# Row maxima of causal attention: which query tiles share a PSUM bank, and in which order their matmuls and searches are issued

## The chip, the cores and the metric

The kernel runs on one core of one Trainium2 chip. The metric is the device time of one execution in microseconds (us), lower is better. Engines are named as in the profile: PE (TensorE matmuls), PEld (TensorE weight loads), DVE (VectorE), ACT (ScalarE), POOL (GpSimd) and SP (SyncE, which issues the DMAs). A PSUM bank holds 512 fp32 columns on 128 partitions; PE writes its results there, DVE and ACT read them.

## The reference, cut to what matters

A block of 2048 tokens by 1024 channels: adaptive layer norm, gated infini-attention with 32 heads of 32 channels, a residual, a second layer norm, a token-mixing MLP, a second residual. The change lies in the attention, which works on four segments of 512 tokens:

```python
for s in range(N):                                   # N = 4 segments, L = 512
    qs, ks, vs = q[:, :, s], k[:, :, s], v[:, :, s]
    logits = jnp.einsum("bhqd,bhkd->bhqk", qs, ks) * scale + mask   # causal
    p = _softmax(logits, axis=-1)
    a_dot = jnp.einsum("bhqk,bhkd->bhqd", p, vs)
    ...                                              # memory read, gate, memory update
```

A softmax row needs the maximum of its logits. The kernel finds it in a pass of its own, for each head and segment: 512 queries, each against the keys up to its own position.

## The kernel before, in words

**Stages.** The first 70 us load inputs and build the first normed segment. From there to about 1035 us runs the attention: a loop over 32 iterations (two passes, eight groups of four heads, two segments each) with four heads in each, so 128 heads in all. The rest is the output product (L733) and the MLP (L863), which the change doesn't touch.

**The loop of the attention (L631 to L655).** Step `n` emits, in this order: `scores(n)`, `maxima(n + 3)`, `values(n - 1)`, and one of four pieces of `project` for a later iteration; beside these come loads, weight splits and other work from a table of due steps (`todo`). `project` computes keys and values (L196) and queries (L204) in fp32 split into a high and a low part, and stacks them by DMA into the tiles `sk`. `scores` computes the transposed logits (L476 to L483) and their exponentials. `values` multiplies by the values (L505) and finishes on DVE (L508 to L513).

**`maxima` (L431 to L456).** For one head the 512 queries are taken in four tiles of 128. Tile i needs the keys of tiles 0 to i: its matmul (L441) has 128·i + 128 columns, so 128, 256, 384 and 512. After each matmul one DVE operation (L442) adds the causal mask, writes the sum back in place and leaves the row maximum in a column of `mx`; the profile shows it as a CUSTOM_DVE operation followed by a short READ_ACCUMULATOR. I call it the search of the tile. Before, the code asks for three tiles of the PSUM tag `s1`, which has two banks: x holds query tile 0 in columns 0 to 127 and query tile 2 in columns 128 to 511, y holds query tile 1, and z query tile 3. The order written down is matmul 0, search 0, matmul 2, search 2, matmul 1, search 1, matmul 3, search 3. After every second head the maxima of both are transposed on PE (L448), negated and split (L450, L451), and four DMAs (L455) put them as two extra rows into `sk`, where the matmuls of `scores` subtract them.

**What sets the order on the chip.** The program is laid out ahead of time by a planner. It takes the instructions in program order as priority, uses its own estimates of their durations, and writes a fixed queue for each engine; a later instruction whose inputs it plans to be ready may be put ahead of an earlier one that it plans to wait. Banks of one tag are handed out by the planner too, to the next tile that asks as soon as it plans one free. On the chip each engine works its queue strictly in order, and an instruction waits where its input or its bank isn't ready yet. Two instructions of different engines on one bank are kept in program order, even where their columns differ.

Other users of the tag `s1`: one in two of the transposes of the first segments (L221, before the loop), the first query projection, and the MLP, long after the loop. The tags `pj` (2 banks), `s2` (2), `pv` (1) and `ms` (1) hold the projections, the scores, the values and the small results.

Of the kernel before, what the change touches and what calls it, by code (L numbers as in the profile page):

```python
# [12 lines left out]
ALU = mybir.AluOpType  # L13
# [16 lines left out]
LEADP, LEADS, NSK = 8, 3, 8  # L30
# [12 lines left out]
LEADS = 3  # L43


def attention_and_mlp(ctx, tc, x, wq, wkv, wo, beta, w1, b1, w2, b2, c, wm_a, wm_b, out):
    nc = tc.nc
    V, A, G, T, SY = nc.vector, nc.scalar, nc.gpsimd, nc.tensor, nc.sync
# [27 lines left out]
    def bank(tag, bufs, name):  # L76
        return psum.tile([P, 512], F32, tag=tag, bufs=bufs, name=name)
# [5 lines left out]
    mask = top.tile([P, L], BF16, name="mask")  # L83
# [194 lines left out]
    for ct in range(NK):  # L278
        for part in range(2):
# [9 lines left out]
            else:  # L289
                for k in range(NK):  # L290
                    T.matmul(scale_ps[:, ct:ct + 1], wm[:, P * k:P * k + P], sc[:, k:k + 1], start=(k == 0),
                             stop=(k == NK - 1), skip_group_check=True)
# [138 lines left out]
    def maxima(t, h):  # L431
        d = st[t]
        if h % 2 == 0:
            d["mx"] = b.tile([P, 2, 4], F32, tag="mx", bufs=2, name=f"mx{t}_{h}")
        mx = d["mx"]
        q, k = d["sk", h][0:96, 0], d["sk", h][0:96, 1]
        x = bank("s1", 2, f"sx_{t}_{h}")
        y = bank("s1", 2, f"sy_{t}_{h}")
        z = bank("s1", 2, f"sz_{t}_{h}")
        for i, o in ((0, x[:, 0:128]), (2, x[:, 128:512]), (1, y[:, 0:256]), (3, z)):  # L440
            T.matmul(o, q[:, 128 * i:128 * i + 128], k[:, 0:128 * i + 128], start=True, stop=True)  # L441
            marks[4 * t + h - LEADS, "V"] = V.tensor_tensor_reduce(  # L442
                o, o, mask[:, 384 - 128 * i:], 1.0, -3.0e38, op0=ALU.add, op1=ALU.max,
                accum_out=mx[:, h % 2, i:i + 1])
        if h % 2 == 0:
            return
        ps = bank("ms", 1, f"nmps{t}_{h}")
        T.transpose(ps[0:8, 0:128], mx.rearrange("p a b -> p (a b)"), ident)  # L448
        nt = [b.tile([8, P], F32R, tag=f"nt{i}", bufs=2, name=f"nt{i}_{t}_{h}") for i in range(2)]
        A.activation(nt[0], ps[0:8, 0:128], AF.Copy, scale=-1.0)  # L450
        V.scalar_tensor_tensor(nt[1], ps[0:8, 0:128], -1.0, nt[0].bitcast(F32), op0=ALU.mult, op1=ALU.subtract)  # L451
        for hh in range(2):
            sk = d["sk", h - 1 + hh]
            for part in range(2):
                SY.dma_start(sk[96 + part:97 + part, 0].bitcast(F32).rearrange("p (b n) -> p b n", n=128),  # L455
                             nt[part][4 * hh:4 * hh + 4].bitcast(F32))  # L456

    marks = {}
# [172 lines left out]
    for n in range(-LEADS, 4 * NI + VL):  # L631
        at(scores, n)
        at(maxima, n + LEADS)
        at(values, n - VL)
        m = n + LEADP
        if 0 <= m + 4 < 4 * NI:
            t = (m + 4) // 4
            if its[t][:2] not in W:
                with tc.issue_after(last_sk[0, 3].ins):
                    load_w(its[t][1], its[t][0])  # L640
        if m >= 8:
            at(project, m)
        if 59 <= m < 67:
            seg, ct = 2 + (m - 59) // 4, 2 * ((m - 59) % 4)
            reload_h(seg, ct)
            reload_h(seg, ct + 1)
        if 4 * NI - 5 <= m < 4 * NI + 3:
            i = m - 4 * NI + 5
            for c in (2 * (i % 4), 2 * (i % 4) + 1):
                wop[c, i // 4] = new_page(f"wo{c}_{i // 4}")  # L650
                if c < 5 or i < 4:
                    SY.dma_start(wop[c, i // 4].bitcast(F32), wos[c, i // 4])
        for f, engines in todo.pop(n, ()):
            with behind(n, engines):
                f()  # L655
# [58 lines left out]
    def product(tt):  # L714

        r = wr_.tile([P, NK, P], F32, tag="otr", bufs=1, name=f"otr{tt}")
        SY.dma_start(r, oT[:, :, P * tt:P * tt + P].rearrange("g p n -> p g n"))
        os_ = ws_.tile([P, 2, D], F32R, tag="ots", bufs=2, name=f"ots{tt}")
        for j in range(2):
            split(os_[:, :, 512 * j:512 * j + 512], r[:, 4 * j:4 * j + 4].rearrange("p a b -> p (a b)"), A, V)  # L720
        x1 = w.tile([P, D], F32, tag="x1", bufs=2, name=f"x1_{tt}")
        load = SY.dma_start(x1, x[P * tt:P * tt + P])
        if tt == 1:
            with tc.issue_after(load.ins):
                for c in range(5, NK):
                    SY.dma_start(wop[c, 1].bitcast(F32), wos[c, 1])

        def half(nh):
            ps = bank("pj", 2, f"po{tt}_{nh}")
            n = 0  # L730
            for ct in range(NK):
                for i, j in ((0, 0), (0, 1), (1, 0)):
                    T.matmul(ps, os_[:, i, P * ct:P * ct + P], wop[ct, nh][:, j], start=(n == 0), stop=(n == 3 * NK - 1))  # L733
                    n += 1
            c0, c1 = 512 * nh, 512 * nh + 512
            V.scalar_tensor_tensor(x1[:, c0:c1], ps, 1.0, x1[:, c0:c1], op0=ALU.mult, op1=ALU.add,
                                   accum_out=x1s[:, 2 * tt + nh:2 * tt + nh + 1])
            if nh:
                kept[tt] = SY.dma_start(x1d[tt], x1)

        return half
# [49 lines left out]
    for products, tt in (((0, 1), 0), ((2,), 1), ((3, 4, 8), 8), ((9,), 9), ((10,), 2), ((11,), 10), ((12,), 3),  # L791
# [5 lines left out]
        for i in products:  # L797
            if i > 1:
                f = product(i)
# [284 lines left out]
```

## Time and profile before

| | us |
|---|---|
| median of 3 runs | 2254.03 |
| lowest and highest of them | 2251.84, 2257.36 |
| the profiled execution | 2248.92 |
| its span, first to last instruction | 2247.2 |
| PE busy in it | 2195.4 |
| DVE busy | 1671.5 |
| ACT busy | 1145.6 |
| POOL busy | 748.6 |

How to read the views: a row of grouped instructions names line, engine, operation, tiles (written <- read), shapes and count; then busy time and mean duration in ns; then the idle time of that engine just before these instructions and what ended it. A row of the timeline has start, duration, engine, line, operation, tiles, shapes and count, and in brackets the engine's idle time before it. A row of the waits has the waiting line, the arrow to what ended the wait, total, number and longest. The tiles of the maxima are called sx, sy and sz; the shapes tell which query tile is meant (96x128, 96x256, 96x384 and 96x512 on PE, 128x128 to 128x512 on DVE).

### The profile page before, as it was taken

Reading aid. Unit: us, or ns where it says so; the run is one execution under the profiler, and the core shown is the slowest. Engines: PE = TensorE matmul, PEld = TensorE weight load, DVE = VectorE, ACT = ScalarE, POOL = GpSimd, SP = SyncE. Lnnn points to the kernel's source line nnn. Section 1 sums busy time; section 2 is a strip of 40 time slices with the busy share of each in tenths; the row PEclk is TensorE's granted clock in tenths of the full one; section 3 lists DMA queues with packets and bytes.
Section 4 is the critical chain, followed back from the end, with each engine's and each line's share of the span. In section 5 each row is a group of like instructions: output and inputs, shape, how many; then the busy total and the mean of one; then the engine's idle time right before and its main releaser. Section 6 shows DMA issues by size and latency. Waiting matters only on the chain.

```text
span 2247.2 us, 38365 instructions
## 1 busy us (share of the span) xinstructions
PE 2195.4 (98%) x13802; PEld 1892.9 (84%) x13802; DVE 1671.5 (74%) x3778; ACT 1145.6 (51%) x2106; POOL 748.6 (33%) x847
## 2 busy tenths in 40 slices
PE   7999999999999999999999999999999999999999
PEld 6879888888988888988888888888888888888887
DVE  6676777766767777655758866788888887868687
ACT  6476867765666656655546633533334242424232
POOL 5166657656666667654001200033330000000000
PEclk9999999999999999999999999999999999999999
DMA  6656565687666566664764587755556541414134
GB/s 263 204 169 174 160 185 161 199 283 239 176 182 207 168 188 193 190 198 164 229 220 151 215 333 262 262 190 221 206 202 238 203 154 57 155 57 146 57 122 150
DMA packets 175186, 423.06 MB, mean 188 GB/s; under 512 B 17524, under 2 KB 71828, under 8 KB 166036
## 3 DMA queue, kind: packets, MB, share of 16 engines
q1 hardware_dynamic: 174996, 420.61, 57.1%
q8 instruction: 110, 1.80, 0.3%
q14 instruction: 80, 0.66, 0.1%
HBM read 244.62 MB, written 125.06 MB: 165 GB/s over the span
## 4 chain that ended last, share of the span: by engine, by line
PE 83%; DVE 7%; DMA 3%; POOL 2%; ACT 2%; issue 2%; SPq 1%; ACTq 0%; DVEq 0%; POOLq 0%
PE mx L863 44%; PE nps L196 11%; PE po L733 8%; PE qps L204 7%; PE pv L505 3%; PE a L476 1%; PE sx L441 1%; PE sz L441 1%; POOL ph L491 1%; DMA wr<-in_w_dram 1%; DVE ac L870 1%; PE a L479 1%; PE rd L413 1%; PE a L483 1%; PE sy L441 1%
## 5 line engine op out<-in xcount | busy, mean ns | idle before, releaser
L863 PE MATMUL mx<-bU,sp 128*128 128x512 f32 x2352 | 534.7, 389 | 1.1 <-DVE ac L870 0.9
L863 PEld LDWEIGHTS mx<-bU,sp 128*128 128x128 f32 x2352 | 441.0, 188 | 94.3 <-issue 1.3
L196 PE MATMUL nps<-wv,h 128*128 128x256 f32 x3072 | 441.7, 284 | 4.7 <-POOL h L126 3.8
L123 ACT CAST sp<-wr 128x384 fp32r<-128x384 f32 (+2 forms) x408 | 217.1, 545 | 430.5 <-PE mx L863 349.6
L491 POOL TENSOR_TENSOR ph<-p,ph 128x640 f16<-128x640 f32 x256 | 378.5, 1499 | 170.2 <-ACT ph L489 169.6
L863 PE MATMUL mx<-bA,sp 128*128 128x512 f32 x1764 | 430.5, 389 | 0.0
L196 PEld LDWEIGHTS nps<-wv,h 128*128 128x128 f32 x3072 | 405.6, 190 | 13.1 <-POOL h L126 5.0
L863 PEld LDWEIGHTS mx<-bA,sp 128*128 128x128 f32 x1764 | 331.1, 188 | 68.8
L126 DVE TENSOR_TENSOR sp<-wr,sp 128x384 fp32r<-128x384 f32 (+2 forms) x408 | 260.1, 648 | 31.5 <-ACT sp L123 31.3
L870 DVE TENSOR_TENSOR ac<-mx,ac 128x512 f32<-128x512 f32 x280 | 189.9, 686 | 85.2 <-PE mx L863 84.8
L204 PE MATMUL qps<-h,wq 128*128 128x512 f32 x768 | 196.3, 397 | 0.0
L489 ACT CAST ph<-p 128x1280 f16<-128x1280 f32 x128 | 160.9, 1257 | 51.6 <-POOL p L487 50.9
L733 PE MATMUL po<-wo,ots 128*128 128x512 f32 x768 | 181.3, 391 | 0.0
L487 POOL TENSOR_SCALAR_AFFINE_SELECT p<-p 128x256 f32<-128x256 f32 x256 | 131.7, 524 | 108.4 <-ACT p L484 54.8
L733 PEld LDWEIGHTS po<-wo,ots 128*128 128x128 f32 x768 | 142.7, 188 | 29.1
L863 PE MATMUL mx<-bB,sp 128*128 128x512 f32 x588 | 164.0, 389 | 0.0
L204 PEld LDWEIGHTS qps<-h,wq 128*128 128x128 f32 x768 | 140.9, 189 | 26.8 <-ACT vp L364 0.3
L442 DVE CUSTOM_DVE_ANT_0 sx<-sx,mask 128x128 f32<-128x128 f32 (+1 forms) x256 | 110.6, 432 | 65.4 <-PE sx L441 63.6
L505 PE MATMUL pv<-vp,ph 128*128 128x97 bf16 (+1 forms) x2560 | 141.9, 202 | 5.2 <-DVE red L512 2.8
L505 PEld LDWEIGHTS <-ph 128*128 128x128 f16 x2560 | 113.6, 98 | 28.7 <-issue 11.9
L863 PEld LDWEIGHTS mx<-bB,sp 128*128 128x128 f32 x588 | 110.4, 188 | 22.9
L870 DVE TENSOR_TENSOR cc<-mx,cc 128x512 f32<-128x512 f32 x140 | 95.0, 685 | 38.3 <-PE mx L863 38.1
(200 smaller groups left out, 3191.7 us busy)
## 6 DMA issues: line engine op xcount, KB each, us to landing
sk<-sg SPq DMA_DIRECT2D x384, 128.0 KB
wr<-in_w_dram SPq DMA_DIRECT2D x28, 1024.0 KB
wr<-in_w_dram SPq DMA_DIRECT2D x32, 768.0 KB
bstu<-ucd SPq DMA_DIRECT2D x28, 768.0 KB
wsp<-wv SPq DMA_DIRECT2D x32, 512.0 KB
rawm<-in_wm_b_dram SPq DMA_DIRECT2D x32, 512.0 KB
wv<-wsp SPq DMA_DIRECT2D x32, 512.0 KB
pcd<-cc SPq DMA_DIRECT2D x14, 1024.0 KB
```

The costliest lines, as they stand in the source:

```text
L123: last_hi[0] = A.copy(hi, src)
L126: lo_eng.tensor_tensor(lo, src, hi.bitcast(F32), op=ALU.subtract)
L196: T.matmul(ps[:, aa], h[:, j, 128 * tt:128 * tt + 128], wt[:, i, o:o + 256], start=(n == 0), stop=(n >= 6 * NK - 2), skip_group_check=True)
L204: T.matmul(ps, wt[:, i, o:o + 128], h[:, j], start=(k + n == 0), stop=(3 * k + n == 3 * NK - 1))
L442: marks[4 * t + h - LEADS, "V"] = V.tensor_tensor_reduce(o, o, mask[:, 384 - 128 * i:], 1.0, -3.0e38, op0=ALU.add, op1=ALU.max, accum_out= ...
L487: G.affine_select(w, w, pattern=[[0, 2], [1, 128]], compare_op=ALU.is_ge, fill=0.0, base=0, channel_multiplier=-1)
L489: marks[n, "A"] = A.copy(ph[:, 0], p32)
L491: marks[n, "G"] = G.tensor_tensor(ph[:, 1, c], p32[:, c], ph[:, 0, c], op=ALU.subtract)
L505: T.matmul(pv[:, i, 0:w], ph[:, part, o:o + 128], d["vp"][:, j, h, 0:w], start=(n == 0), stop=(n == 19), skip_group_check=True)
L733: T.matmul(ps, os_[:, i, P * ct:P * ct + P], wop[ct, nh][:, j], start=(n == 0), stop=(n == 3 * NK - 1))
L863: T.matmul(ps, ops[q][:, i, P * k:P * k + P], b[:, j], start=(m == 0 and first), stop=(m == 3 * nk - 1), skip_group_check=True)
L870: V.tensor_tensor(d, ps, d, op=ALU.add)
```

## The change

The four tiles of queries are issued in three groups, each in a bank tile of its own: tiles 0 and 1 together (named sx, columns 0 to 127 and 128 to 383), tile 2 alone (sy, columns 0 to 383), tile 3 alone (sz, 512 columns). In the first group both matmuls are issued before both searches. The operations, their shapes and their number stay the same.

```diff
-        x = bank("s1", 2, f"sx_{t}_{h}")
-        y = bank("s1", 2, f"sy_{t}_{h}")
-        z = bank("s1", 2, f"sz_{t}_{h}")
-        for i, o in ((0, x[:, 0:128]), (2, x[:, 128:512]), (1, y[:, 0:256]), (3, z)):
-            T.matmul(o, q[:, 128 * i:128 * i + 128], k[:, 0:128 * i + 128], start=True, stop=True)
-            marks[4 * t + h - LEADS, "V"] = V.tensor_tensor_reduce(
-                o, o, mask[:, 384 - 128 * i:], 1.0, -3.0e38, op0=ALU.add, op1=ALU.max,
-                accum_out=mx[:, h % 2, i:i + 1])
+        for tiles in ((0, 1), (2,), (3,)):
+            s = bank("s1", 2, f"s{'xxyz'[tiles[-1]]}_{t}_{h}")
+            outs = [(i, s[:, 128 * i * (len(tiles) - 1):][:, 0:128 * i + 128]) for i in tiles]
+            for i, o in outs:
+                T.matmul(o, q[:, 128 * i:128 * i + 128], k[:, 0:128 * i + 128], start=True, stop=True)
+            for i, o in outs:
+                marks[4 * t + h - LEADS, "V"] = V.tensor_tensor_reduce(
+                    o, o, mask[:, 384 - 128 * i:], 1.0, -3.0e38, op0=ALU.add, op1=ALU.max,
+                    accum_out=mx[:, h % 2, i:i + 1])
```

`marks` keeps the last search of each step; work from the table of due steps that names "V" is queued on DVE behind it. It is the search of tile 3 in both versions.

## The prediction

> **What bounds the kernel now.** I read the page first: the busy time of each engine against the span.
>
> ```profile
> span 2247.2 us, 38365 instructions
> ## 1 busy us (share of the span) xinstructions
> PE 2195.4 (98%) x13802; PEld 1892.9 (84%) x13802; DVE 1671.5 (74%) x3778; ACT 1145.6 (51%) x2106; POOL 748.6 (33%) x847
> ```
>
> PE is busy 98% of the span. A change that neither adds nor removes matmuls can only win back PE's idle time or add to it. Next I cut the span at the end of the attention, 1035 us; the columns are busy time and instructions of each engine, then granted clock, DMA share and GB/s.
>
> ```profile
> core 0: us, PE busy (x) PEld busy (x) DVE busy (x) ACT busy (x) POOL busy (x), PEclk, DMA share, GB/s
> 70.00:1035.00 965.00, 935.31 (x8089) 847.03 (x8088) 680.21 (x2018) 626.04 (x1148) 597.22 (x699) 1.00 0.64 193
> 1035.00:2248.00 1213.00, 1207.53 (x5393) 998.01 (x5391) 944.68 (x1652) 476.30 (x880) 112.86 (x81) 1.00 0.51 181
> ```
>
> From 70 to 1035 us PE is idle for 965.00 - 935.31 = 29.7 us. That is all that any gain of this stage can come from, 1.3% of the time. The clock is full, so no gain comes from there. DVE is idle for 965.00 - 680.21 = 284.8 us: it has room, but it works in order, so it can still be late at one place. The waits of PE in this stage tell what ends its idle time; the longest rows are:
>
> ```profile
> PE a L476 <- DMA sk<-nt: 5.4, 4, 2.1
> PE sx L441 <- DVE mx L442: 5.1, 12, 1.2
> PE sz L441 <- DVE mx L442: 3.3, 7, 1.3
> PE sy L441 <- DVE mx L442: 3.0, 6, 0.7
> PE pv L505 <- DVE red L512: 2.8, 2, 1.5
> ```
>
> The matmuls of the maxima wait for searches, 5.1 + 3.3 + 3.0 = 11.4 us in 25 waits. That is the largest single reason of PE's idle time here, and the change is at these waits. The grouped rows, with shapes kept apart, say which query tile waits:
>
> ```profile
> L441 PE MATMUL sz<-sk 96*128 96x512 f32 x128 | 54.1, 422 | 3.5 <-DVE mx L442 3.3
> L441 PE MATMUL sx<-sk 96*128 96x384 f32 x128 | 47.7, 373 | 3.8 <-DVE mx L442 3.7
> L441 PE MATMUL sy<-sk 96*128 96x256 f32 x128 | 41.7, 326 | 3.0 <-DVE mx L442 3.0
> L441 PE MATMUL sx<-sk 96*128 96x128 f32 x128 | 31.9, 250 | 2.2 <-DVE mx L442 1.4 <-DMA sk<-sg 0.7
> ...
> L441 PEld LDWEIGHTS sx<-sk 96*128 96x128 f32 x256 | 48.7, 190 | 13.3 <-DVE mx L442 9.7 <-DVE am L417 0.9
> ```
>
> So tile 0 waits 1.4 us, tile 1 3.0, tile 2 3.7, tile 3 3.3. The last row is the idle time of the weight loads of tiles 0 and 2 together: 9.7 us behind searches, against 1.4 + 3.7 = 5.1 on the matmul rows. The end of a matmul is modelled, so the time lost lies between the two.
>
> What such a wait looks like, from the timeline, in one head:
>
> ```profile
> 437.46 1.23 DVE L126 TENSOR_TENSOR wv<-rawv,wv 128x512 fp32r<-128x512 f32 x1
> ...
> 437.94 0.23 PE L441 MATMUL sx<-sk 96*128 96x128 f32 x1
> ...
> 438.00 0.33 PE L441 MATMUL sy<-sk 96*128 96x256 f32 x1
> ...
> 439.15 1.34 DVE L126 TENSOR_TENSOR wv<-rawv,wv 128x512 fp32r<-128x512 f32 x1
> ...
> 440.42 0.29 DVE L442 CUSTOM_DVE_ANT_0 sx<-sx,mask 128x128 f32<-128x128 f32 x1
> 440.63 0.13 DVE L442 DVE_READ_ACCUMULATOR2_ANT mx<- 128x1 f32 x1
> 440.63 0.46 DVE L442 CUSTOM_DVE_ANT_0 sy<-sy,mask 128x256 f32<-128x256 f32 x1
> 440.82 0.19 PEld L441 LDWEIGHTS sx<-sk 96*128 96x128 f32 x1 [1.39 <-DVE mx L442]
> 440.82 0.44 PE L441 MATMUL sx<-sk 96*128 96x384 f32 x1 [1.15 <-DVE mx L442]
> ...
> 441.10 4.30 PE L204 MATMUL qps<-h,wq 128*128 128x512 f32 x18
> ```
>
> The matmuls of tiles 0 and 1 are done at 438.3. DVE is still splitting weights (L126, two operations of 1.3 us) and searches tile 0 only at 440.42 to 440.71. The matmul of tile 2 writes another part of the same bank, so it starts at 440.82, 0.11 us after the search. It stands in PE's queue ahead of 18 query projections, which need nothing from it, so PE is idle for 1.15 us.
>
> This head also shows that the planner already runs tile 1 ahead of tile 2, though the code writes 0, 2, 1, 3.
>
> **The change part by part.** *What stays.* Four matmuls, four weight loads, four searches and four reads of the accumulator for each of the 128 heads, with the same columns; no DMA is added, removed or moved past another in the code. Tile 1 moves to columns 128 to 383, tile 2 to columns 0 to 383. Does a search cost more at another start column? The rows of DVE:
>
> ```profile
> L442 DVE CUSTOM_DVE_ANT_0 sz<-sz,mask 128x512 f32<-128x512 f32 x128 | 89.4, 698 | 38.0 <-PE sz L441 37.7
> L442 DVE CUSTOM_DVE_ANT_0 sx<-sx,mask 128x384 f32<-128x384 f32 x128 | 72.7, 568 | 28.7 <-PE sx L441 27.8
> L442 DVE DVE_READ_ACCUMULATOR2_ANT mx<- 128x1 f32 x512 | 71.6, 140 | 0.0
> L442 DVE CUSTOM_DVE_ANT_0 sy<-sy,mask 128x256 f32<-128x256 f32 x128 | 55.7, 435 | 25.7 <-PE sy L441 25.1
> L442 DVE CUSTOM_DVE_ANT_0 sx<-sx,mask 128x128 f32<-128x128 f32 x128 | 37.9, 296 | 36.6 <-PE sx L441 35.8
> ```
>
> From 296 to 435, 568 and 698 ns the steps are 139, 133 and 130 ns for each 128 columns, though only the 568 starts at column 128. The start column costs nothing; the searches stay at about 2.0 us a head.
>
> *What is removed.* Today four matmuls of a head can each wait for a search: tile 0 and tile 1 for the two banks that the head before leaves (last by its searches 2 and 3), tile 2 for search 0 in its own bank, tile 3 for search 1, whose bank it takes over. After the change tile 1 goes into tile 0's bank with no search between them, and tile 2 into the other bank, free after search 3 of the head before. Tile 3 takes the first group's bank, free after search 1. So the wait of tile 2 for search 0 is gone, and three waits of a head are left instead of four. Its price is the 3.7 us of the 96x384 row, or up to 9.7 by the weight loads, if nothing takes its place. I take 3.7: in the head above the two measures differ only by 1.39 against 1.15, and 9.7 holds tile 0's waits as well.
>
> *What is moved.* The wait for search 3 of the head before passes from tile 1 to tile 2. Today it costs 3.0 us. It comes later in the head, which speaks for less; but the planner puts a matmul just where it plans the bank free, so it is as tight as before. Ends 0 and 3.0 us saved; I take 0. Tile 3 still waits for search 1, as today (3.3 us). Where the wait of tile 2 hid it, it now shows: in the head above tile 2 would run beside the pair, and tile 3, if planned just behind search 1, would stop PE until search 1 ends at 441.09. Ends 3.3 us saved, or all of the 3.7 taken up again; I take 0. Tile 0's wait (1.4 us) is for search 2 of the head before in both versions; 0.
>
> *What is added.* Search 0 now waits for matmul 1 as well, since both use one bank. Behind it in DVE's queue stand whatever the planner puts there: weight splits that the projections need, the end of `values`, `pq`. A head in which matmul 1 follows at once shows the cost:
>
> ```profile
> 372.12 0.22 PE L441 MATMUL sx<-sk 96*128 96x128 f32 x1
> ...
> 372.18 0.33 PE L441 MATMUL sy<-sk 96*128 96x256 f32 x1
> ...
> 372.38 0.30 DVE L442 CUSTOM_DVE_ANT_0 sx<-sx,mask 128x128 f32<-128x128 f32 x1 [2.30 <-PE sx L441]
> ...
> 372.60 0.47 DVE L442 CUSTOM_DVE_ANT_0 sy<-sy,mask 128x256 f32<-128x256 f32 x1
> ```
>
> Matmul 0 ends at 372.34, search 0 starts 0.04 later. Matmul 1 ends at 372.51, so search 0 would start at 372.55, 0.17 us later than now. For 128 heads that is 21.8 us on DVE. Its cover is DVE's idle time, 284.8 us in this stage, and here 2.30 us just before the search; I take 0. If the cover were gone, up to 21.8 us would come on top (rival 2). That the two matmuls stand side by side costs PE nothing: here they start 0.06 us apart.
>
> [...]
>
> *The sum.* -3.7 us. The profiled execution took 2248.92, of which the span is 2247.2 and 1.7 lies around it: 2248.92 - 3.7 = 2245.2. It was 5.1 us faster than the median of the runs, 2254.03, and I forecast the median: 2254.03 - 3.7 = 2250.3, so 2250, 0.16% less. What a measurement of this kernel can tell from no change is about 0.3%, 6.8 us, so the forecast counts as no change.
>
> **The rivals.** *1. More than one wait goes.* Three searches can follow each other, so the banks come free earlier at every point, and the maxima of a head are done sooner. Then all 11.4 us go: 2242.6. If the two maxima rows also reach `sk` sooner, the 5.4 us that `scores` waits for their DMA (`sk<-nt`) go too: 2237.2. I put this rival at 2240. For it: every remaining wait has a whole search of at least 0.57 us (tile 2), 0.70 (tile 3) or 0.30 + 0.43 (the pair) running beside it, where today tile 1's wait has only search 0 (0.30) and tile 2's only search 1 (0.43). Against it: at 440.42 DVE was late through weight splits of 1.3 us, not through searches, and that lateness stays.
>
> *2. The pair holds VectorE up (slower).* Search 0 starts 0.17 us later in each head, and the in-order queue of DVE passes it on to what PE waits for. For it: four of the five rows of PE's waits above end with DVE, so PE does run into a late DVE in this stage. Against it: DVE is idle 30% of the stage. At full price it is 2254.03 - 3.7 + 21.8 = 2272.1. It decides the sign from the point where more than 3.7 / 0.17 = 22 of the 128 heads pass the delay on, and it is beyond 0.3% from (3.7 + 6.8) / 0.17 = 62 heads on. A matmul 1 that the planner sets some instructions behind matmul 0 makes the delay longer for that head, so fewer heads are enough.
>
> *3. The change does nothing.* The planner already runs 0, 1, 2, 3, and the removed wait comes back at tile 3, behind search 1. Then the time stays at 2254.
>
> **How the numbers follow.** Forecast, one wait less, 2250: 0.31. Rival 1, about 2240: 0.28. Rival 2, slower, 2261 (62 heads) to 2272: 0.30. Rival 3, 2254: 0.11. A new plan shuffles neighbours in both directions, which is why rivals 1 and 2 keep so much. Faster by over 0.3% is rival 1, 0.28; within 0.3% are the forecast and rival 3, 0.42; slower by over 0.3% is rival 2, 0.30. The range goes from rival 1 with the DMA wait, 2237, to just under the full price of rival 2, 2270; beyond each end I leave about 0.1. The forecast's own range is 2247 to 2254, from 3.7 + 3.0 saved to nothing saved.
>
> **What would show it.** Right: the 96x384 row of PE loses most of its 3.7 us of idle time behind searches, the rows of 96x128 and 96x512 keep about 1.4 and 3.3, PE's idle time between 70 and 1035 us falls from 29.7 to about 26, and search 0 starts only after matmul 1 in every head. Rival 1: the rows of all four tiles fall below 1 us each and PE's idle time below 20 us. Rival 2: PE's idle time rises, ended by DVE lines other than the searches (L126, L512, L387), and the idle time of DVE before search 0 grows above its 36.6 us by 15 us or more. Rival 3: the 96x512 row grows by what the 96x384 row loses. Wrong altogether would be a difference after 1035 us, where PE was idle 5.5 us and no instruction of the change runs.

## The result and the profile after

| | before | after |
|---|---|---|
| median of 6 runs each, us | 2254.77 | 2239.82 |
| lowest and highest, us | 2250.21, 2258.01 | 2237.27, 2242.11 |
| the profiled execution, us | 2248.92 | 2241.52 |
| its span, us | 2247.2 | 2239.8 |

The changed kernel takes 0.9935 of the time before, 95% interval 0.9920 to 0.9949: 15 us faster, where 2250 was forecast. The two profiled executions differ by only 7.4 us; why is shown below. After line 441 the changed kernel's line numbers are one higher.

The head of the page after, to set against the one of before:

```profile
span 2239.8 us, 38394 instructions
## 1 busy us (share of the span) xinstructions
PE 2192.1 (98%) x13802; PEld 1897.4 (85%) x13802; DVE 1672.5 (75%) x3778; ACT 1147.5 (51%) x2106; POOL 748.9 (33%) x847
```

The engines' instructions are the same in number. PE is busy 3.3 us less (2195.4 before), and its idle time, span less busy time, went from 51.8 to 47.7 us: only part of the difference is idle time. The two stages after, with the columns of before:

```profile
70.00:1035.00 965.00, 940.02 (x8161) 857.12 (x8160) 686.22 (x2032) 634.60 (x1158) 602.57 (x705) 0.99 0.65 194
1035.00:2240.00 1205.00, 1199.28 (x5323) 991.83 (x5321) 939.74 (x1636) 469.68 (x870) 107.79 (x74) 1.00 0.51 181
```

PE's idle time up to 1035 us went from 29.7 to 965.00 - 940.02 = 25.0 us, behind 1035 us it stayed (5.5 and 5.7). What ended PE's waits in the attention, after, longest first:

```profile
PE sx L441 <- DMA sk<-nt: 5.7, 1, 5.7
PE sz L441 <- DVE mx L443: 5.2, 5, 1.7
PE a L477 <- DMA sk<-nt: 2.6, 3, 1.3
PE sx L441 <- DMA sk<-sg: 1.9, 2, 1.0
PE sy L441 <- DVE mx L443: 1.4, 3, 0.7
...
PE rd L413 <- DVE pq L387: 0.6, 1, 0.6
```

Waits for searches fell from 25 with 11.4 us to 8 with 5.2 + 1.4 = 6.6 us. The row of `pv` behind `red`, 2.8 us before, is no longer among the long ones. One wait of 5.7 us is new: near 518 to 524 us PE stands until rows of `sk` have landed. By query tile, matmuls and weight loads after:

```profile
L441 PE MATMUL sz<-sk 96*128 96x512 f32 x128 | 55.3, 432 | 5.3 <-DVE mx L443 5.2
L441 PE MATMUL sy<-sk 96*128 96x384 f32 x128 | 46.2, 361 | 1.7 <-DVE mx L443 1.4
L441 PE MATMUL sx<-sk 96*128 96x256 f32 x128 | 43.2, 338 | 0.0
L441 PE MATMUL sx<-sk 96*128 96x128 f32 x128 | 31.4, 246 | 8.1 <-DMA sk<-nt 5.7 <-DMA sk<-sg 1.9 <-DVE red L511 0.4
...
L441 PEld LDWEIGHTS sx<-sk 96*128 96x128 f32 x256 | 43.1, 193 | 13.2 <-DMA sk<-nt 5.9 <-DVE mx L443 1.3 <-issue 1.1
L441 PEld LDWEIGHTS sz<-sk 96*128 96x128 f32 x128 | 24.5, 192 | 8.4 <-DVE mx L443 7.0
L441 PEld LDWEIGHTS sy<-sk 96*128 96x128 f32 x128 | 24.5, 191 | 3.9 <-DVE mx L443 3.3
```

The weight loads of tiles 1 and 3 before, to set beside them:

```profile
L441 PEld LDWEIGHTS sy<-sk 96*128 96x128 f32 x128 | 24.4, 191 | 6.2 <-DVE mx L442 4.5 <-DVE rdd L415 0.2
L441 PEld LDWEIGHTS sz<-sk 96*128 96x128 f32 x128 | 24.3, 190 | 7.3 <-DVE mx L442 6.2
```

By the matmul rows, tile 1 (96x256) never waits now, tile 2 (96x384) waits less, tile 3 (96x512) more. The searches on DVE after:

```profile
L443 DVE CUSTOM_DVE_ANT_0 sz<-sz,mask 128x512 f32<-128x512 f32 x128 | 89.0, 696 | 41.1 <-PE sz L441 40.6
L443 DVE CUSTOM_DVE_ANT_0 sy<-sy,mask 128x384 f32<-128x384 f32 x128 | 73.5, 574 | 20.8 <-PE sy L441 20.2
...
L443 DVE CUSTOM_DVE_ANT_0 sx<-sx,mask 128x256 f32<-128x256 f32 x128 | 56.0, 438 | 1.3
L443 DVE CUSTOM_DVE_ANT_0 sx<-sx,mask 128x128 f32<-128x128 f32 x128 | 38.0, 297 | 58.9 <-PE sx L441 58.6
```

The durations are those of before within 6 ns. DVE's idle time before search 0 rose from 36.6 to 58.9 us, before search 1 it fell from 25.7 to 1.3, before search 2 from 28.7 to 20.8: in all from 129.0 to 122.1.

**Why the profiles differ by less than the medians.** The granted clock after is 0.99 in the attention, before it was 1.00. In stretches of 3.4 or 6.8 us the granted clock is 0.50, and matmuls follow each other more slowly: in the stretch of the kernel after that stands below, the query projections (L204) start 0.43 us apart, just behind it 0.23. One of before, then one of after, each with the stretch ahead of it and the one behind:

```profile
125.70:129.10 3.40, 2.35 (x19) 1.58 (x19) 3.40 (x15) 2.33 (x2) 2.14 (x2) 0.99 0.16 39
129.10:132.50 3.40, 3.40 (x22) 2.86 (x19) 1.69 (x9) 2.92 (x9) 0.80 (x2) 0.50 0.77 275
132.50:135.90 3.40, 3.40 (x18) 2.87 (x18) 2.66 (x9) 3.40 (x7) 1.27 (x2) 1.00 0.11 32
```

```profile
461.70:465.10 3.40, 2.30 (x25) 1.44 (x24) 2.21 (x6) 3.40 (x7) 1.88 (x5) 0.99 0.91 333
465.10:471.90 6.80, 6.23 (x17) 4.98 (x18) 6.70 (x17) 4.13 (x8) 6.27 (x5) 0.50 0.97 386
471.90:475.30 3.40, 3.40 (x23) 2.75 (x22) 0.60 (x1) 0.58 (x1) 2.23 (x3) 1.00 1.03 422
```

Between 75 us and the end of the attention there are 6.8 us at half clock in the profiled execution before and 20.5 us in the one after. Executions of one kernel differ in this: of 27 of the kernel before, the six with a mean clock of 0.992 or 0.993 took 2256.9 to 2258.5 us and the two at 0.997 took 2250.0 and 2250.3. The profiled one of before had 0.998, after 0.995. So the pair of profiles understates the gain; the medians don't. The clock is not the gain itself: of the same 27 executions the 14 at 0.995 to 0.997 took 2250.0 to 2255.8 us, and the six of the changed kernel, all at 0.995 to 0.997 too, 2237.3 to 2242.1.

### The profile page after: what moved, and what is told of

Read it like the earlier page. It is cut to its first block, busy times and chain, and to the rows that moved or that the text cites. A ratio compares the mean times of both kernels' runs of the same rounds, so it can differ in the third digit from the quotient of the medians.

```text
span 2239.8 us, 38394 instructions
## 1 busy us (share of the span) xinstructions
PE 2192.1 (98%) x13802; PEld 1897.4 (85%) x13802; DVE 1672.5 (75%) x3778; ACT 1147.5 (51%) x2106; POOL 748.9 (33%) x847
## 4 chain that ended last, share of the span: by engine, by line
PE 86%; DVE 4%; DMA 4%; ACT 3%; POOL 2%; issue 1%; SPq 0%; ACTq 0%; DVEq 0%; POOLq 0%
PE mx L864 48%; PE nps L196 12%; PE qps L204 7%; PE po L734 6%; PE pv L506 3%; PE sz L441 1%; PE a L477 1%; PE sx L441 1%; POOL ph L492 1%; PE up L423 1%; PE rd L413 1%; DVE wv L126 1%; PE a L480 1%; PE sy L441 1%; PE a L484 1%
## 5 line engine op out<-in xcount | busy, mean ns | idle before, releaser
L196 PE MATMUL nps<-wv,h 128*128 128x256 f32 x3072 | 438.1, 283 | 3.2 <-POOL h L126 3.2
L196 PEld LDWEIGHTS nps<-wv,h 128*128 128x128 f32 x3072 | 406.1, 190 | 10.1 <-POOL h L126 4.2
L204 PE MATMUL qps<-h,wq 128*128 128x512 f32 x768 | 199.0, 402 | 0.1
L204 PEld LDWEIGHTS qps<-h,wq 128*128 128x128 f32 x768 | 142.5, 192 | 28.1 <-ACT vp L364 0.4
L443 DVE CUSTOM_DVE_ANT_0 sx<-sx,mask 128x128 f32<-128x128 f32 (+1 forms) x256 | 94.0, 367 | 60.3 <-PE sx L441 58.6
```

What stands on the lines that cost most here:

```text
L196: T.matmul(ps[:, aa], h[:, j, 128 * tt:128 * tt + 128], wt[:, i, o:o + 256], start=(n == 0), stop=(n >= 6 * NK - 2), skip_group_check=True)
L204: T.matmul(ps, wt[:, i, o:o + 128], h[:, j], start=(k + n == 0), stop=(3 * k + n == 3 * NK - 1))
L443: marks[4 * t + h - LEADS, "V"] = V.tensor_tensor_reduce(o, o, mask[:, 384 - 128 * i:], 1.0, -3.0e38, op0=ALU.add, op1=ALU.max, accum_out= ...
```

## The experiments

Theory W: a head's matmuls had four waits for a search and now have three, and each bank comes free earlier; that is the gain. Rivals: the order of the searches (O), how tiles share banks (B, C), S, that any edit makes the planner write other queues, whose neighbours fall luckily or not, and H, that the gain is only when search 0 or its neighbours come on DVE.

**Four waits in other forms.** `order_0123` keeps the banks and writes the order 0, 1, 2, 3:

```diff
-        for i, o in ((0, x[:, 0:128]), (2, x[:, 128:512]), (1, y[:, 0:256]), (3, z)):
+        for i, o in ((0, x[:, 0:128]), (1, y[:, 0:256]), (2, x[:, 128:512]), (3, z)):
```

> Banks and waits as before (four waits for a search in each head), only the order written down is 0, 1, 2, 3. Theory W (a head's matmuls have one wait for a search less, and every bank comes free earlier): nothing changes, ratio to before 0.998 to 1.002, idle time of the L441 matmuls behind searches about 11 us as before. Rival O (the gain is that tile 1 is searched ahead of tile 2): ratio about 0.9935. Rival S (any edit makes the planner write another order, and its neighbours fall luckily or not): a move of up to 0.7% either way.

Measured: 2255.8 us, ratio to before 1.0004 (0.9995 to 1.0012). This run alone says little on the order: in the kernel before, the planner already had the matmuls as 0, 1, 2, 3 in 121 of the 128 heads. The next runs say more.

`pair_serial` is the changed kernel with matmul 1 behind search 0:

```diff
             for i, o in outs:
                 T.matmul(o, q[:, 128 * i:128 * i + 128], k[:, 0:128 * i + 128], start=True, stop=True)
-            for i, o in outs:
                 marks[4 * t + h - LEADS, "V"] = V.tensor_tensor_reduce(
```

> The banks of the changed kernel, but matmul 1 is issued after search 0, so it waits for it: four waits in a head again. Theory W: the gain is gone, ratio to before 0.998 to 1.003, and matmul 1 shows 3 us or more of idle time behind search 0. Rival B (the gain comes from how the tiles share the banks, not from both matmuls ahead): 0.9935. Rival S: up to 0.7% either way, with no link to the idle time behind searches.

Measured: 2257.57 us, ratio 1.0015 (1.0004 to 1.0025). With the same tiles in a bank and matmul 1 no longer ahead of search 0, the gain is gone. The planner also changed the order: matmul 2 stands ahead of matmul 1 in 118 of 128 heads. That order is not what lost the gain, since `pair_02` below has it in all 128 heads. Its PE waits for searches:

```profile
PE sx L441 <- DVE mx L442: 4.0, 8, 0.8
PE sy L441 <- DVE mx L442: 3.8, 6, 1.5
...
PE sz L441 <- DVE mx L442: 2.9, 6, 1.2
```

20 waits with 10.7 us, much as before the change. Matmul 1 waits 3.0 us of it, as expected.

`four_banks` gives each tile a bank tile of its own:

```diff
-        for tiles in ((0, 1), (2,), (3,)):
-            s = bank("s1", 2, f"s{'xxyz'[tiles[-1]]}_{t}_{h}")
+        for tiles in ((0,), (1,), (2,), (3,)):
+            s = bank("s1", 2, f"s{'wxyz'[tiles[-1]]}_{t}_{h}")
```

> Each of the four tiles takes a bank tile of its own, so no matmul writes a bank in which an earlier part is still to be searched, but each waits for the search two places before it: four waits in a head. Theory W: no gain, ratio 0.998 to 1.003, idle time behind searches about 11 us. Rival C (what cost time before was the second use of one bank, tile 2 behind search 0): about 0.9935 to 0.996. Rival S: up to 0.7% either way.

Measured: 2256.01 us, ratio 0.9999 (0.9990 to 1.0008). Its queues turned out to be those of `order_0123`, instruction by instruction on every engine: tile 2 gets tile 0's bank either way. So it says nothing on rival C, but shows how well the same queues repeat: 2255.8 and 2256.01.

**Three waits in other forms.** `pair_02` puts tiles 0 and 2 together:

```diff
-        for tiles in ((0, 1), (2,), (3,)):
+        for tiles in ((0, 2), (1,), (3,)):
...
-            outs = [(i, s[:, 128 * i * (len(tiles) - 1):][:, 0:128 * i + 128]) for i in tiles]
+            outs = [(i, s[:, 128 * (i > 0) * (len(tiles) - 1):][:, 0:128 * i + 128]) for i in tiles]
```

> Tiles 0 and 2 share a bank with both matmuls ahead, tiles 1 and 3 take a bank each: three waits in a head, as in the changed kernel, but the pair holds its bank for 0.30 + 0.57 us and the single tile for only 0.44. Theory W: most of the gain, ratio 0.993 to 0.997, idle time behind searches 5 to 8 us. Rival O (searching 1 ahead of 2): ratio 1.00. Rival S: up to 0.7% either way.

Measured: 2237.5 us, ratio 0.9921 (0.9907 to 0.9934). Its waits for searches:

```profile
PE sy L441 <- DVE mx L443: 2.9, 6, 0.8
PE sx L441 <- DVE mx L443: 0.6, 1, 0.6
PE sz L441 <- DVE mx L443: 0.5, 1, 0.5
```

8 waits with 4.0 us. This pair is as good as the one of the change, and a little better than theory W expected of it (0.993 to 0.997, and 5 to 8 us). Its matmuls stand as 0, 2, 1, 3 in all heads, those of the changed kernel as 0, 1, 2, 3, and both gain: the order is not the gain.

`swap_search` is the changed kernel with search 1 ahead of search 0:

```diff
-            for i, o in outs:
+            for i, o in outs[::-1]:
                 marks[4 * t + h - LEADS, "V"] = V.tensor_tensor_reduce(
```

> The changed kernel with the two searches of the pair in the other order: 1, then 0. Waits and banks are the same three for each head; only the queues are laid out anew. Theory W (one wait less, banks free earlier): as the changed kernel, ratio to before 0.992 to 0.995. Rival S (chance of the new layout): may fall anywhere from 0.990 to 1.003. Rival H (the gain is only that search 0 or its neighbours come at another time on DVE): away from 0.9935 by more than 0.003.

Measured: 2253.89 us, ratio 0.9989 (0.9972 to 1.0006), and its runs spread from 2241.75 to 2259.14. Theory W missed: three waits, no gain. Rivals S and H both allow it, and this run doesn't tell them apart. The profile shows where some of it is:

```profile
PE sx L441 <- DMA sk<-sg: 8.9, 5, 5.2
...
PE sz L441 <- DVE mx L443: 4.0, 5, 1.7
...
PE sx L441 <- DVE mx L443: 2.2, 3, 1.6
...
PE sy L441 <- DVE mx L443: 1.2, 3, 0.6
```

The waits for searches stayed few (11, with 7.4 us); the first matmuls of a head wait 8.9 us for the stacks of queries and keys, where the changed kernel has 1.9. PE's idle time (span less busy time) is 56.5 us, against 47.7 in the changed kernel, its busy time 2196.4 against 2192.1. The spread goes with the clock in part: the fastest execution had a mean clock of 0.997, the slowest 0.991. The stacks are not the whole answer: `pair_02` waits 4.4 us for them and gained. `pair_serial` waits 7.7 us for them, so its loss may be layout in part as well.

`pair_last` has the groups in the order 2, 3, then 0 and 1; `pair02_mid` has 1, then 0 and 2, then 3:

```diff
-        for tiles in ((0, 1), (2,), (3,)):
+        for tiles in ((2,), (3,), (0, 1)):
```

```diff
-        for tiles in ((0, 2), (1,), (3,)):
+        for tiles in ((1,), (0, 2), (3,)):
...
```

> The same three groups in the order 2, 3, then 0 and 1. Three waits in a head, but the pair now waits for the search of tile 2 and the next head for those of tile 3 and of the pair. Theory W: ratio 0.992 to 0.996. Rival S: anywhere from 0.990 to 1.003. If the short tiles have to come first for the gain (maxima ready early), ratio 0.998 to 1.00.

> Tiles 0 and 2 in one bank with both matmuls ahead, but after tile 1: groups 1, then 0 and 2, then 3. Three waits in a head. Theory W: ratio 0.991 to 0.995, as with the other pairs. Rival S: anywhere from 0.990 to 1.003.

Measured: 2245.05 us, ratio 0.9961 (0.9947 to 0.9974), and 2243.25 us, ratio 0.9954 (0.9936 to 0.9971). They missed the ranges of theory W by 0.0001 and 0.0004. Both keep over half of the gain, whichever tiles make the pair and wherever it stands.

**Fewer waits still.** `five_groups` takes five bank tiles for two heads: with the second head, tile 1 of both shares one.

```diff
...
-        for tiles in ((0, 1), (2,), (3,)):
...
+        for name, tiles in (("x", ((h, 0, 0), (h, 2, 128))), ("y", ((h - 1, 1, 0), (h, 1, 256))), ("z", ((h, 3, 0),))):
+            if name == "y" and h % 2 == 0:
+                continue
...
```

> Two heads take five bank tiles in place of six: tiles 0 and 2 of a head share one, tile 3 takes one, and tile 1 of both heads shares one that is filled with the second head. So 2.5 waits a head. Theory W, if each wait per head is worth some 15 us: a further gain, ratio 0.986 to 0.990. If the gain was only that tile 2 stood behind search 0: no further gain, 0.992. If tile 1 of the first head coming a step late makes its maxima late: 0.995 or slower. Rival S: anywhere from 0.988 to 1.003.

Measured: 2243.7 us, ratio 0.9953 (0.9937 to 0.9970). No further gain, with 8 waits of 4.6 us left for searches. So a wait less is not worth 15 us each time. Some 0.995 was expected if tile 1 of the first head, coming late, makes its maxima late; whether that is the reason was not tried by itself.

**How much is the layout?** `before_ml41` and `after_ml41` move the work of the late modulation by one step, `before_wo66` and `after_wo66` that of the output weights; the maxima stay as they are in each kernel.

```diff
-ML0 = 40
+ML0 = 41
```

```diff
-WO0 = 65
+WO0 = 66
```

> The kernel before with the loads and products of the late modulation one step later in the loop (ML0 41 for 40): the maxima are untouched, the queues are laid out anew. Theory W (three waits for a search in place of four are the gain): stays with the kernels of four waits, ratio 0.997 to 1.004. Rival S (the layout decides, and the change only drew a good one): may come out anywhere, 0.992 to 1.006.

> The changed kernel with the same shift (ML0 41). Theory W: about 0.5% ahead of before_ml41, that is 12 us, give or take 6 us for the layout. Rival S: no more ahead of it than chance, 0 give or take 8 us.

> The kernel before with the preparation of the output weights one step later (WO0 66 for 65). Theory W: ratio 0.997 to 1.004. Rival S: anywhere from 0.992 to 1.006.

> The changed kernel with the same shift (WO0 66). Theory W: about 12 us ahead of before_wo66, give or take 6 us. Rival S: 0 give or take 8 us.

| layout | four waits, us | three waits, us | difference |
|---|---|---|---|
| as given | 2254.77 | 2239.82 | -15.0 |
| ML0 41 | 2262.51, ratio 1.0043 (1.0030 to 1.0057) | 2235.51, ratio 0.9933 (0.9921 to 0.9946) | -27.0 |
| WO0 66 | 2245.24, ratio 0.9967 (0.9955 to 0.9980) | 2245.22, ratio 0.9967 (0.9955 to 0.9980) | 0.0 |

Both have a part, and neither forecast the sizes. Theory W expected 12 us give or take 6 in each new layout, so 27 and 0 both miss it; 27 also lies outside what rival S alone gave, 0 give or take 8. `before_ml41` lies 0.0003 above the range of theory W and `before_wo66` 0.0003 below it. Put together, with the ratio to before of each kernel (a layout that came out twice counted once) and PE's waits for searches in its profile:

| kernels | ratios | waits for searches, number | the same, us | PE busy, us | PE idle (span less busy), us |
|---|---|---|---|---|---|
| four waits: before, order_0123 and four_banks, pair_serial, before_ml41, before_wo66 | 1, 1.0002, 1.0015, 1.0043, 0.9967 | 18 to 25 | 7.3 to 11.4 | 2195.4 to 2207.0 | 48.5 to 56.0 |
| three waits: after, pair_02, swap_search, pair_last, pair02_mid, after_ml41, after_wo66 | 0.9935, 0.9921, 0.9989, 0.9961, 0.9954, 0.9933, 0.9967 | 8 to 13 | 4.0 to 7.7 | 2191.1 to 2196.4 | 41.6 to 56.5 |

The means are 1.0005 and 0.9951: 0.54% or 12 us apart. The kernels of a group scatter by 0.27% and 0.23% (standard deviations, 5 to 6 us), so the difference of the means is known to about 0.35%, or 8 us, either way (95%, taking these few layouts for a random draw, which they are not quite). Theory W holds for the mean, rival S for the spread: a single layout can give the gain back whole or nearly double it.

The last two columns show where the mean gain lies. The means of the groups are 6.3 us apart in PE's busy time (2199.5 and 2193.2) and 4.9 us in its idle time (52.4 and 47.5), with the same matmuls. The busy time holds stretches at half clock, which are described above. With half of PE's busy time in those taken off, as an estimate from the granted 0.50 of what full clock would take, it is 2187.0 to 2190.6 us in the kernels with four waits and 2179.2 to 2183.7 in those with three. There the groups don't overlap, and `swap_search` (2182.3) stands with the three waits: what it lost, it lost in idle time and at half clock. Part of the shorter busy time shows in the row of the key and value projections (L196): 437.4 to 442.7 us with four waits, 430.3 to 439.1 with three.

## Why the prediction was right or wrong

The time lies in the range (2237 to 2270) and the sign of the sum was right. The likeliest case was not: the forecast was 2250 and no change to speak of; what came is the time of rival 1, 2240, without the signs that were named for it. The rows of tiles 2 and 3 stay above 1 us, and PE's idle time from 70 to 1035 us is 25.0 us, not below 20. About 26 was named for the forecast. So the idle time came out as forecast and the time did not, and that the time still lies in the range is partly luck. Point by point:

- **PE's idle time in the attention is all that can be won: the step that failed.** The idle time there fell by 4.7 us (29.7 to 25.0), close to the sum of 3.7, though in part by other waits than it named. But PE's busy time, which the prediction held fixed because the matmuls stay, fell as well: by 3.3 us between the two profiles, though the one after had 13.7 us more at half clock, and by 6.3 us between the means of the two groups of kernels, where idle time gave 4.9. How the same matmuls came to take less is not shown, nor whether a busy row, in which the ends of matmuls are modelled, holds waiting. Behind 1035 us the idle time stayed (5.5 and 5.7), as forecast.
- **The clock is full: not quite.** The 1.00 of that row is rounded; 6.8 us of the stage ran at half clock.
- **Tile 2's wait goes, 3.7 us: right in kind.** Its row fell from 3.7 to 1.4 us, now for the head before.
- **Tile 1's wait passes to tile 2 without getting smaller (0 taken, up to 3.0): wrong.** Tile 1's 3.0 us are gone, and tile 2 shows 1.4 in all, so 1.6 were saved, about halfway between the ends. Rival 1 named a likely reason, a longer search running beside each wait that is left; that this is the reason was not tried by itself.
- **Tile 3 keeps its wait: wrong by 1.9 us**, 3.3 to 5.2. That is what rival 3 spoke of, in part. Three of its five waits, with 3.1 us of the 5.2, stand in heads where the planner put search 2 ahead of search 1, for which tile 3 waits; it did so in 56 of the 128 heads.
- **Tile 0's wait stays at 1.4: wrong.** No wait for a search is left in its matmul row.
- **The pair makes search 0 late by 0.17 us in each head, 21.8 us on DVE, covered: right.** Search 0 starts after matmul 1 in all 128 heads. Measured are 58.9 - 36.6 = 22.3 us, though that the numbers lie so close is luck: 5.7 us of the 58.9 come from the one stop near 524 us, and 22 heads had search 0 behind matmul 1 already before. DVE as a whole idles less before searches, since search 1 no longer waits (25.7 to 1.3). Rival 2's mechanism is there, and no cost of it shows. The pair has two of the four matmuls in one bank with no search between them, and the kernel with it is the faster one (ratio 0.9935); so is `pair_02` (0.9921). The other two groups still change banks.
- **The sum, -3.7: too small.** It priced one query tile by the idle time of the matmul rows. On those rows all waits for searches fell by 11.4 - 6.6 = 4.8 us. On the weight-load rows they fell from 9.7 + 4.5 + 6.2 = 20.4 to 1.3 + 7.0 + 3.3 = 11.6, by 8.8. The prediction held that the time lost lies between the two measures. The measured 15 us, and the 12 of the mean, lie above both.
- **Lateness passed on to others was counted at nothing in the sum.** (Rival 1 had the last of these.) `pv` behind `red` (2.8) has gone from the long rows, `rd` behind `pq` fell from 1.7 to 0.6, `scores` behind the maxima's DMA from 5.4 to 2.6. All but the last are waits for DVE operations that aren't searches. Against this stands the new wait of 5.7 us for a DMA.
- **The profiled execution of before stood 5.1 us below the median of its runs**, and the prediction left it there without a reason. It had few stretches at half clock, as shown above.

What stays open: how the 15 us of this pair divide between the wait and the luck of the layout. The mean over layouts says about 12 plus or minus 8 for the wait. Open too is in what way PE's busy time got shorter, why `swap_search` waits so much for its stacks, and why WO0 66 levels both kernels. No kernel tried is clearly better than the changed one: `pair_02` (0.9921) and `after_ml41` (0.9933) have intervals that overlap its own.

## What to carry to other kernels

Where two engines hand a bank back and forth, count the waits in a round, not only the time of one wait: putting two short matmuls ahead of both their searches took one hand-over of four away, and the engine that waited longer in front of the first search (DVE, 58.9 us for 36.6) waited less in front of all four (122.1 us for 129.0). Don't take the idle time of a busy engine as the upper end of what its waits cost: here TensorE's busy time, with the same matmuls, fell by more in the mean of the layouts (6.3 us) than its idle time (4.9 us). Where a planner writes the queues, measure a change of 0.5% in two or three layouts before you believe its size: here the same edit gave 0, 15 and 27 us.

## What the runs showed of the hardware

The stretches at half clock were not expected. Between 75 us and the end of the attention the profile before has two of 3.4 us (from 129.1 and 327.0 us), the one after three of 6.8 us (from 250.0, 465.1 and 523.1 us), all with a granted clock of 0.50. Not all stand behind an idle PE: PE was busy for 2.35 of the 3.40 us before the one at 129 us and for 2.30 before the one at 465 us, in rows quoted above. The one at 523 us does, in the wait of 5.7 us: from 519.7 to 523.1 us no matmul runs. In the 27 runs of the kernel before, 0.997 against 0.992 or 0.993 of mean clock went with some 7 us. What sets off such a stretch is not shown; no run here tries it by itself.
